# Set attention and a hard-swish layer on one core: the order and the issuers of the first loads, and half of a weight cast by a transfer

## The chip, the cores and the metric

The kernel runs on one core of one Trainium2 chip. The metric is the device time of one execution, in microseconds; lower is better. Time before: a median of 312.26 us over 6 runs (311.8 to 313.66).

## The reference

Two attention blocks with 32 inducing points, and then a feed-forward layer with a hard-swish, on x of 4 batches of 12480 tokens by 128 channels.

```
h   = mab(inducing, x)          # per batch: softmax over 12480 tokens, 32 x 128
y   = mab(x, h)                 # softmax over 32 points, 12480 x 128
mab(q, kv): a = softmax(q @ kv.T / sqrt(128));  return a @ kv
u   = y.reshape(49920, 128) @ w_in          # 128 x 2048
out = (u * clip(u + 3, 0, 6) / 6) @ w_out   # 2048 x 128
```

All inputs and the output are float32.

## The kernel before

The kernel does not run the layer over its 2048 hidden columns for each token. From each batch's 32 inducing outputs it makes small coefficient tables (a linear part BD and a quadratic part Cq), and per chunk of 512 tokens it multiplies features of the token by them. A path that computes everything directly stands at the end and is entered only where a test of the values fails.

A batch is cut into six groups of 2048 tokens (128 partitions by 16 tokens) and a small one of 192 tokens (48 partitions by 4, group NF = 6). For each batch there are two stages. The first reads the batch (casts x to bf16 as xb, transposes it on TensorE into pt, copies pt to xT, multiplies by the inducing points to s, takes the exponential a, and sums hnd += a x). The second makes the coefficients and then the output. For batches 1 to 3 the first stage is laid between the output steps of the batch before; for batch 0 it stands alone at the start, and this is where the change is made. The schedule is written out by hand: every engine runs its instructions in the order in which the program gives them.

The steps of the opening, in the order in which they appear, with their lines:

- L106: SyncE loads the table of inducing points into I_sb.
- L110 load_x: loads one group of x into a tile of type fp32r, by GpSimd's queue (L122), in one request or in two halves. L125 loads group 0 in halves. L164 builds the identity on GpSimd, and L165 then loads the small group and groups 1 to 5 in one go. Group 5 of batch 0 lies in an output buffer (tile x), the others in five buffers xr.
- L172 warm(n): n matmuls on zeros in TensorE. L181 transposes I_sb into I_T.
- L185 to L220: GpSimd writes constants (memsets, copies, an iota), and L229 load_weights loads w_in_r and w_out_r (1 MB each).
- L340 a_first: batch 0 goes through in pieces of half a group. The small group is the third of the 13 pieces. Per turn k, the loop does transpose(k + 1), weights(k) (s and its exponential, L378 and L385), cast(k + 3) and add(k - 1) (hnd, L392, and the running sums of a on VectorE, dacc, then dlast for the last four pieces). Five pieces before the end GpSimd folds dacc (L415). A group's buffer is given to a group of batch 1 once its last half has been added (load_next, L418); from group 2 on those loads are held back until load_held (L132), which waits with a small copy, seen, for one of the d transfers.
- L627 c_first: the coefficients of batch 0. ScalarE casts w_in to w_in_b in two halves and w_out to w_out_b in four quarters (cast_w, L637), between its squares sq (L579) of the products dpm (L568). TensorE accumulates cp (L588) from sq and w_out_b, block by block (16 blocks of 128 hidden columns); every fourth block's square is done by VectorE (L576, L577). SyncE spreads dk into the tiles d (L763).
- L905: the loop over the chunks, which writes out (L844).

Of the kernel before, what the change touches and what calls it, by code (L numbers as in the profile page):

```python
# [40 lines left out]
def kernel(  # L41
# [39 lines left out]
    with ExitStack() as es:  # L81
# [21 lines left out]


        I_sb = const.tile([M, C], FP32, name="I_sb")
        nc.sync.dma_start(I_sb[:, :], inducing[:, :])  # L106

        xs, xbs = {}, {}

        def load_x(b, g, cuts=(0, TG)):  # L110
            t0, p, n = groups[g]
            src = x[b, t0 : t0 + p * n, :].rearrange("(p i) c -> p i c", i=n)
            if n < TG:
                t = xlast.tile([P, n, C], FP32R, name="xl")
            elif b == 0 and g == XBUF:

                t = osp.tile([P, TG, C], FP32R, name="x5", tag="os")
            else:
                t = xin.tile([P, TG, C], FP32R, name="xr")
            for lo, hi in zip(cuts, cuts[1:]):  # L120
                lo, hi = min(lo, n), min(hi, n)
                nc.gpsimd.dma_start(t[:p, lo:hi, :], src[:, lo:hi, :])  # L122
            xs[(b, g)] = t

        load_x(0, 0, (0, 8, 16))  # L125

        held = []
        NF = NGR - 1 if rest else NGR
# [29 lines left out]
        def load_weights():  # L158
            w_out = moe_w_out.rearrange("(kb kp) c -> kp kb c", kp=P)
            nc.gpsimd.dma_start(w_in_r[:, :], moe_w_in[:, :])  # L160
            nc.gpsimd.dma_start(w_out_r[:, :, :], w_out)


        make_identity(nc, ident[:, :])  # L164
        for g in (NF, *range(1, XBUF + 1)):  # L165
            load_x(0, g, (0, 8, 16) if g in (1, XBUF - 1, XBUF) else (0, TG))
        wake = const.tile([P, 512], BF16, name="wake")
        nc.vector.memset(wake[:, :], 0.0)
        ident_b = const.tile([P, P], BF16, name="ident_b")
# [2 lines left out]
        def warm(n):  # L172

            wp = psF.tile([P, 512], FP32, name="wp", tag="fb")
            for _ in range(n):
                nc.tensor.matmul(wp[:, :], lhsT=wake[:, :P], rhs=wake[:, :])
# [3 lines left out]
        itp = psF.tile([P, 512], FP32, name="itp", tag="fb")  # L180
        nc.tensor.transpose(itp[:, :M], I_sb[:, :], ident[:M, :M])  # L181
        nc.vector.tensor_copy(I_T[:, :], itp[:, :M])
        warm(8)

        eng = nc.gpsimd  # L185
        ones = const.tile([P, P], FP32, name="ones")
# [5 lines left out]
        for q in range(4):  # L192
            eng.memset(blk_f[32 * q : 32 * q + 32, 32 * q : 32 * q + 32], 1.0)
            eng.memset(one4_f[32 * q : 32 * q + 32, q : q + 1], -1.0)
        blk = const.tile([P, P], FP32R, name="blk")
        eng.tensor_copy(blk[:, :], blk_f[:, :])
        one4 = const.tile([P, SL], FP32R, name="one4")
# [25 lines left out]
        def half_rows():  # L223
# [2 lines left out]
            nc.vector.tensor_scalar(half_of[:, :], half_of[:, :], 3.0, 1.0 / 12.0, op0=ALU.is_equal, op1=ALU.mult)  # L226
            nc.vector.tensor_scalar_add(half_of[:, :], half_of[:, :], -1.0 / 6.0)

        load_weights()  # L229


# [108 lines left out]
        def a_first():  # L340

            st = S[0]
            pieces = [(g, h, h + 8) for g in range(XBUF + 1) for h in (0, 8)]
            pieces.insert(2, (NF, 0, SL))
            last = len(pieces) - 1
            a1s = {}

            def cast(k):
                g, lo, hi = pieces[k]
                p = groups[g][1]  # L350
                if lo == 0:
                    xbs[(0, g)] = xbin.tile([P, TG, C], BF16, name="xb")
                xb, xf = xbs[(0, g)], xs[(0, g)]
                if hi - lo == 8 and (lo == 0 or k == last):
                    cuts = [(nc.scalar.copy, lo, lo + 4), (nc.vector.tensor_copy, lo + 4, hi)]
                else:
                    cuts = [(nc.scalar.copy, lo, hi)]
                for eng, i, j in cuts:
                    eng(xb[:p, i:j, :], xf[:p, i:j, :].bitcast(FP32))

            def transpose(k):
                g, lo, hi = pieces[k]
                t0, p, n = groups[g]
                step = 4 if k == last else 8
                for i in range(lo, hi, step):
                    j = min(i + step, hi)
                    pt = side_bank(0, [P, 1024], BF16, "pt")
                    for q in range(i, j):
                        nc.tensor.transpose(pt[:, (q - i) * p : (q - i + 1) * p], xbs[(0, g)][:p, q, :], ident_b[:p, :p])
                    eng = nc.scalar.copy if k == last and i > lo else nc.vector.tensor_copy  # L370
                    eng(st["xT"][:, t0 + i * p : t0 + j * p], pt[:, : (j - i) * p])

            def weights(k):
# [14 lines left out]
            def add(k):  # L388
                g, lo, hi = pieces[k]
                p, w, a1 = groups[g][1], (hi - lo) * M, a1s[k]  # L390
                for q in range(lo, hi):
                    nc.tensor.matmul(  # L392
                        st["hnd"][:M, :C],
                        lhsT=a1[:p, (q - lo) * M : (q - lo + 1) * M],
                        rhs=xs[(0, g)][:p, q, :],
                        start=(k == 0 and q == lo),
                        stop=(k == last and q == hi - 1),
                    )
                f = a1[:p, :w].bitcast(FP32)
                d = st["dacc"][:p, lo * M : hi * M]  # L400
                if g == 0:
                    nc.vector.tensor_copy(d, f)
                elif k == last - 3:
                    st["dlast"] = cst.tile([P, 8 * M], FP32, name="dlast")
                    nc.vector.tensor_copy(st["dlast"][:, :], f)
                elif k > last - 3:
                    nc.vector.tensor_add(st["dlast"][:, :], st["dlast"][:, :], f)
                    if k == last:
                        c_red(0, st["dlast"][:, :], P, 8)
                else:  # L410
                    nc.vector.tensor_add(d, d, f)
                if k == last - 4:
                    d = st["dacc"]
                    for h in (8, 4, 2, 1):
                        nc.gpsimd.tensor_add(d[:, : h * M], d[:, : h * M], d[:, h * M : 2 * h * M])  # L415
                    st.setdefault("dred", []).append(d[:, :M])
                if hi == groups[g][2]:
                    load_next(0, g)  # L418

# [16 lines left out]
        def c_red(b, src, p, n):  # L436
            st = S[b]
            st["reds"] = st.get("reds", -1) + 1
            dred = cst.tile([P, M], FP32, name=f"dred{st['reds']}")
            nc.vector.tensor_reduce(  # L440
                dred[:p, :], src.rearrange("p (s m) -> p m s", m=M), axis=AX.X, op=ALU.add
            )
            st.setdefault("dred", []).append(dred[:p, :])
# [183 lines left out]
        def c_first():  # L627
# [2 lines left out]
            nc.scalar.copy(w_in_b[:, : F // 2], w_in_r[:, : F // 2].bitcast(FP32))  # L630
            c_den(0)
            nc.scalar.copy(w_in_b[:, F // 2 :], w_in_r[:, F // 2 :].bitcast(FP32))
            c_HT(0)
            warm(2)

            def cast_w(i, j):
                nc.scalar.copy(w_out_b[:, i:j, :], w_out_r[:, i:j, :].bitcast(FP32))  # L637
# [16 lines left out]
            for jb in range(3, 7):  # L654
                sg(jb)
                cs(jb - 3)
            cast_w(8, 12)
            sg(7)
            b_f(0, 0)
            cs(4)  # L660
# [4 lines left out]
            c_hs(0)  # L665
            b_base(0, 0, 1)
            cs(6)
            cast_w(12, 16)
            sq(10)
            cs(7)  # L670
            sq(11)
# [445 lines left out]
```

## Time and profile before

| what | value |
|---|---|
| median of 6 runs | 312.26 us |
| the profiled execution | 313.36 us, its span 311.5 us |
| TensorE matmul busy | 299.0 us, 96% of the span |
| VectorE, ScalarE busy | 235.6 us, 231.8 us |
| GpSimd busy | 35.5 us |
| moved by transfers | 66.69 MB |
| granted TensorE clock, mean | 0.994 |

The span runs from the first to the last instruction; the execution's own time has a little around it. Times in the profile are those of one execution. A busy share is an average over the whole span, in which the opening of some 45 us is quite different from the rest. In the views of single instructions a row gives the start, the duration, the engine, the line, the operation and, in brackets, how long the engine had been idle and what it had waited for.

### The profile page before, as it was taken

To read this page: it belongs to the slowest core of one execution; us is meant where nothing else is said; L and a number is where in the kernel's file an instruction comes from. 1 tells how busy PE (TensorE), PEld (TensorE's weight loads), DVE (VectorE), ACT (ScalarE), POOL (GpSimd) and SP (SyncE) were. 2 spreads that over 40 slices of the span, in tenths; PEclk is the share of its full clock that TensorE was granted. 3 is DMA by queue.
4 is the path that set the end of the run, shared out by engine and by line. 5 is a ranking of instruction groups with operands and counts; after the bars stand their busy time and mean duration, and the time that the engine had idled before them with its cause. 6 is when DMAs were issued, how large, how long until landed. Compare 5 with 4: busy or idle time off the path is not lost.

```text
span 311.5 us, 9606 instructions
## 1 busy us (share of the span) xinstructions
PE 299.0 (96%) x3923; PEld 233.8 (75%) x3929; DVE 235.6 (76%) x543; ACT 231.8 (74%) x425; POOL 35.5 (11%) x82
## 2 busy tenths in 40 slices
PE   8899999999999999999999999999999999999991
PEld 3687678887676878888767877888867786777781
DVE  1797796977883868878796668787888487888882
ACT  3778999886589678886679849888658945777760
POOL 7611301021100010101100000100000001000000
PEclk9999999999999999999999999999999999999997
DMA  6999496998963452899965525555255335466672
GB/s 215 393 397 356 103 374 213 310 320 238 387 210 93 142 178 65 294 298 318 336 208 188 176 53 171 182 187 172 51 187 170 142 88 189 161 222 211 215 250 97
DMA packets 25089, 66.69 MB, mean 214 GB/s; under 512 B 3168, under 2 KB 17536, under 8 KB 19408
## 3 DMA queue, kind: packets, MB, share of 16 engines
q0 software_dynamic: 9232, 46.83, 43.6%
q1 hardware_dynamic: 15808, 19.19, 22.6%
q8 instruction: 32, 0.52, 0.7%
q14 instruction: 17, 0.14, 0.1%
HBM read 27.67 MB, written 25.56 MB: 171 GB/s over the span
## 4 chain that ended last, share of the span: by engine, by line
PE 74%; ACT 11%; DVE 5%; DMA 4%; issue 2%; POOL 1%; ACTq 0%; DVEq 0%; POOLq 0%
PE op L816 27%; PE bp L776 11%; PE op L800 7%; PE hnd L290 6%; ACT sq L579 6%; PE pt L268 5%; DMA xr<-in_x_dram 4%; PE cp L588 4%; PE s L276 2%; PE pp L747 2%; ACT TF L783 2%; PE ep L703 2%; PE sp L717 1%; PE dpm L568 1%; PE lp L540 1%
## 5 line engine op out<-in xcount | busy, mean ns | idle before, releaser
L783 ACT ACTIVATE TF<-bp 128x512 bf16<-128x512 f32 (+1 forms) x200 | 117.3, 599 | 38.7 <-PE rp L736 20.9
L816 PE MATMUL op<-Cq,TF 128*128 128x128 bf16 (+1 forms) x800 | 109.3, 223 | 0.0
L816 PE MATMUL op<-Cq,TD 128*128 128x128 bf16 (+1 forms) x800 | 105.9, 219 | 0.0
L832 DVE TENSOR_TENSOR os<-op,r_all 128x512 f32<-128x512 f32 (+1 forms) x100 | 68.4, 684 | 18.9 <-PE op L816 17.8
L816 PEld LDWEIGHTS <-TF 128*128 128x128 bf16 (+1 forms) x800 | 50.5, 98 | 33.5 <-issue 24.8
L776 PE MATMUL bp<-xT,W 128*128 128x512 bf16 (+1 forms) x197 | 74.0, 376 | 0.1
L792 DVE TENSOR_TENSOR TD<-TF,d 128x1024 bf16<-128x1024 bf16 (+1 forms) x100 | 66.8, 668 | 1.0 <-DMA d<-dk 0.6
L816 PEld LDWEIGHTS <-TD 128*128 128x128 bf16 (+1 forms) x800 | 61.4, 98 | 0.7
L800 PE MATMUL op<-BD,nf 128*128 128x512 f32 (+1 forms) x100 | 53.3, 533 | 0.5 <-DVE os L832 0.4
L579 ACT ACTIVATE sq<-dpm 128x512 bf16<-128x512 f32 x60 | 35.2, 641 | 4.3 <-PE dpm L568 2.0
L259 ACT CAST xb<-xr 128x1024 bf16<-128x1024 f32 x36 | 37.6, 1056 | 0.0
L737 DVE RECIPROCAL r_all<-rp 128x4 f32<-128x4 f32 (+1 forms) x100 | 17.7, 177 | 24.3 <-PE rp L736 23.9
L736 PE MATMUL rp<-one,nf 128*128 128x4 f32 (+1 forms) x100 | 34.5, 345 | 0.4
L269 DVE COPY xT<-pt 128x1024 bf16<-128x1024 bf16 (+1 forms) x42 | 25.8, 618 | 8.3 <-PE pt L268 7.8
L844 POOL DMA_DIRECT2D out_dram<-os x21 | 11.3, 537 | 142.7 <-DVE os L832 136.0
L290 PE MATMUL hnd<-xr,a 128*32 128x128 f32 x288 | 24.2, 226 | 0.0
L754 ACT ACTIVATE dk<-pp 128x512 bf16<-128x512 f32 (+1 forms) x28 | 15.7, 560 | 10.4 <-PE pp L747 10.4
L268 PE MATMUL pt<-ident_b,xb 128*128 128x128 bf16 x300 | 23.3, 218 | 0.0
L776 PEld LDWEIGHTS <-W 128*128 128x128 bf16 x200 | 19.5, 97 | 5.0 <-issue 3.4
L588 PE MATMUL cp<-w_out_b,sq 128*128 128x128 bf16 x256 | 22.7, 220 | 0.5 <-ACT sq L579 0.5
L568 PE MATMUL dpm<-dH,w_in_b 128*128 128x512 bf16 x62 | 22.7, 381 | 0.0
L510 PE MATMUL gp<-HTr,w_in_r 128*128 128x32 f32 x64 | 21.3, 358 | 0.3 <-ACT HTr L488 0.3
(127 smaller groups left out, 407.5 us busy)
## 6 DMA issues: line engine op xcount, KB each, us to landing
xr<-in_x_dram POOLq DMA_DIRECT2D x20, 1024.0 KB, 8.0
out_dram<-os POOLq DMA_DIRECT2D x18, 1024.0 KB, 4.4
d<-dk SPq DMA_DIRECT2D x96, 128.0 KB, 3.8
out_dram<-os SPq DMA_DIRECT2D x5, 1024.0 KB, 4.1
xr<-in_x_dram POOLq DMA_DIRECT2D x6, 512.0 KB, 5.6
x<-in_x_dram POOLq DMA_DIRECT2D x2, 512.0 KB, 13.5
w_in_r<-in_moe_w_in_dram POOLq DMA_DIRECT2D x1, 1024.0 KB, 13.5
w_out_r<-in_moe_w_out_dram POOLq DMA_DIRECT2D x1, 1024.0 KB, 16.3
```

What stands on the lines that cost most here:

```text
L259: eng(xb[:p, lo:hi, :], xs[(b, g)][:p, lo:hi, :].bitcast(FP32))
L268: nc.tensor.transpose(pt[:, (i - lo) * p : (i - lo + 1) * p], xb[:p, i, :], ident_b[:p, :p])
L290: nc.tensor.matmul(st["hnd"][:M, :C], lhsT=a1[:p, i * M : (i + 1) * M], rhs=xs[(b, g)][:p, i, :], start=(g == 0 and i == 0), stop=(g == NG ...
L579: nc.scalar.activation(sq[:, :], dpm[:, :], ACT.Square)
L588: nc.tensor.matmul(st["cp"][:, k * C : (k + 1) * C], lhsT=sq[:, k * P : (k + 1) * P], rhs=w_out_b[:, jc, :], start=(jc == 0 and k == 0), s ...
L736: nc.tensor.matmul(rp[:p, :SL], lhsT=nf[:, j * p : (j + 1) * p], rhs=one4[:, :])
L776: nc.tensor.matmul(bp[:, :w], lhsT=st["W"][:, k].rearrange("p m i -> p (m i)"), rhs=st["xT"][:, c0 : c0 + w],)
L783: nc.scalar.activation(st[("x", c)][:, k, :w], bp[:, :w], ACT.Exp, scale=scale)
L792: nc.vector.tensor_mul(u[:, :, :w], t[:, :, :w], d[:, :w].unsqueeze(1).to_broadcast([P, 2, w]))
L800: nc.tensor.matmul(op[:p, :], lhsT=st[("nf", g)][:, j * p : (j + 1) * p], rhs=st["BD"][:, :], start=True, stop=False, skip_group_check=True,)
L816: nc.tensor.matmul(op[:p, s * C : (s + 1) * C], lhsT=T[k][:, s * p : (s + 1) * p], rhs=st["Cq"][:, k, :], start=False, stop=(s == SL - 1 a ...
L832: nc.vector.tensor_mul(ot[:p, j * SL : (j + 1) * SL, :], op[:p, :].rearrange("p (s c) -> p s c", c=C), r_all[:p, b, c, :].unsqueeze(2).to_ ...
```

## The change

The opening gets another order of loads, and one half of a cast another place.

1. Group 0's first half is loaded by SyncE, as plain float32, into an output buffer x0. ScalarE and VectorE cast it from there to bf16, and VectorE copies it into the fp32r tile that TensorE reads for hnd. The table of inducing points is loaded by ScalarE's queue instead.
2. GpSimd loads the second half of group 0, builds the identity, loads the first half of group 1, writes half of its constants, loads the second half of group 1, writes the rest, and then loads groups 2 to 5 in halves, the small group, and the weights.
3. The small group becomes the last of the 13 pieces. The finer cuts that the last piece had stay with the last half of group 5. The folding of dacc on GpSimd now follows the first half of group 4 and not the second half of group 3.
4. The warming run behind the transpose of I_sb has 5 matmuls, not 8.
5. The second half of w_out_b (blocks 8 to 15) is made by a transfer from w_out_r to w_out_b on GpSimd's queue, which casts on the way; the two casts of ScalarE that did it go.

```diff
         I_sb = const.tile([M, C], FP32, name="I_sb")
-        nc.sync.dma_start(I_sb[:, :], inducing[:, :])
...
         def load_x(b, g, cuts=(0, TG)):
...
-            if n < TG:
+            if cuts[0]:
+                t = xs[(b, g)]
+            elif n < TG:
...
-                nc.gpsimd.dma_start(t[:p, lo:hi, :], src[:, lo:hi, :])
+                if (b, g, lo) == (0, 0, 0):
+                    x0 = osp.tile([P, TG, C], FP32, name="x0", tag="os")
+                    nc.sync.dma_start(x0[:, lo:hi, :], src[:, lo:hi, :])
+                    xs["x0"] = x0
+                else:
+                    nc.gpsimd.dma_start(t[:p, lo:hi, :], src[:, lo:hi, :])
             xs[(b, g)] = t
         load_x(0, 0, (0, 8, 16))
+        nc.scalar.dma_start(I_sb[:, :], inducing[:, :])
...
         make_identity(nc, ident[:, :])
-        for g in (NF, *range(1, XBUF + 1)):
-            load_x(0, g, (0, 8, 16) if g in (1, XBUF - 1, XBUF) else (0, TG))
+        load_x(0, 1, (0, 8))
...
-        warm(8)
+        warm(5)
...
             eng.memset(one4_f[32 * q : 32 * q + 32, q : q + 1], -1.0)
+        load_x(0, 1, (8, 16))
...
+        for g in range(2, XBUF + 1):
+            load_x(0, g, (0, 8, 16))
+        load_x(0, NF)
         load_weights()
...
-            pieces.insert(2, (NF, 0, SL))
+            pieces.append((NF, 0, SL))
...
-                if hi - lo == 8 and (lo == 0 or k == last):
+                if hi - lo == 8 and (lo == 0 or k == last - 1):
...
-                    eng(xb[:p, i:j, :], xf[:p, i:j, :].bitcast(FP32))
+                    eng(xb[:p, i:j, :], xs["x0"][:, i:j, :] if k == 0 else xf[:p, i:j, :].bitcast(FP32))
+                if k == 0:
+                    nc.vector.tensor_copy(xf[:, lo:hi, :], xs["x0"][:, lo:hi, :])
...
-                step = 4 if k == last else 8
+                step = 4 if k == last - 1 else 8
...
+                elif k < last - 3:
+                    nc.vector.tensor_add(d, d, f)
                 elif k == last - 3:
                     st["dlast"] = cst.tile([P, 8 * M], FP32, name="dlast")
                     nc.vector.tensor_copy(st["dlast"][:, :], f)
-                elif k > last - 3:
-                    nc.vector.tensor_add(st["dlast"][:, :], st["dlast"][:, :], f)
-                    if k == last:
-                        c_red(0, st["dlast"][:, :], P, 8)
                 else:
-                    nc.vector.tensor_add(d, d, f)
+                    nc.vector.tensor_add(st["dlast"][:p, :w], st["dlast"][:p, :w], f)
...
+                if k == last:
+                    c_red(0, st["dlast"][:, :], P, 8)
...
             nc.scalar.copy(w_in_b[:, F // 2 :], w_in_r[:, F // 2 :].bitcast(FP32))
+            nc.gpsimd.dma_start(w_out_b[:, FB // 2 :, :], w_out_r[:, FB // 2 :, :].bitcast(FP32))
             c_HT(0)
...
-            cast_w(8, 12)
             sg(7)
...
-            cast_w(12, 16)
             sq(10)
```

More of the change, by code (lines that the diff above doesn't have):

```diff
@@ L369, in transpose @@
                         nc.tensor.transpose(pt[:, (q - i) * p : (q - i + 1) * p], xbs[(0, g)][:p, q, :], ident_b[:p, :p])
-                    eng = nc.scalar.copy if k == last and i > lo else nc.vector.tensor_copy
+                    eng = nc.scalar.copy if k == last - 1 and i > lo else nc.vector.tensor_copy
                     eng(st["xT"][:, t0 + i * p : t0 + j * p], pt[:, : (j - i) * p])
```

## The prediction
> **What bounds the kernel now.** I read the page's slices first, then the chain that ended last for the first 60 us, then the order of time and the busy time by stretch over the same part.
>
> ```profile
> PE   8899999999999999999999999999999999999991
> ACT  3778999886589678886679849888658945777760
> DMA  6999496998963452899965525555255335466672
> ```
>
> TensorE is busy nearly everywhere, so the question is what stands ahead of its steady state. The busy time by stretch (sum, then PE, PEld, DVE, ACT, POOL, granted clock, DMA share, GB/s) splits the run:
>
> ```profile
> 3.00:21.70 18.70, 16.73 (x242) 12.85 (x242) 11.85 (x31) 12.12 (x22) 9.99 (x30) 1.00 1.09 385
> 27.88:38.98 11.10, 10.28 (x109) 7.52 (x111) 8.71 (x19) 10.61 (x22) 2.38 (x5) 1.00 0.61 179
> 45.00:290.00 245.00, 243.26 (x3213) 191.08 (x3213) 190.00 (x430) 187.59 (x345) 19.30 (x36) 1.00 0.62 200
> ```
>
> From 45 us on PE is busy 243.26 of 245.00 us. Whatever the opening of the kernel loses or wins arrives at the end one for one. The opening has two bounds: the transfers (share 1.09, 385 GB/s) while batch 0 comes in, and ScalarE (10.61 of 11.10 us) while the first coefficients are made. The chain (start, us, what) says the same:
>
> ```profile
> 3.57 2.64 POOL xr L122 x5
> 6.21 13.00 DMA xr<-in_x_dram
> 19.23 1.05 ACT xb L359
> ...
> 32.73 0.50 ACT w_out_b L637
> ...
> 35.20 0.50 ACT w_out_b L637
> ```
>
> Thirteen microseconds of the path are one wait for x. The last two casts of w_out are on the path as well, 0.50 us each.
>
> ```profile
> 0.76 0.40 SPq L106 DMA_DIRECT2D I_sb<-in_inducing_dram  x1
> 1.28 1.24 POOL L122 DMA_DIRECT2D xr<-in_x_dram  x2 [0.83 <-POOLq L1101]
> 12.71 0.62 ACT L359 CAST xb<-xr 128x512 bf16<-128x512 f32 x1 [1.17 <-DMA xr<-in_x_dram]
> 21.79 0.62 ACT L359 CAST xb<-x 128x512 bf16<-128x512 f32 x1
> 27.88 0.62 ACT L637 CAST w_out_b<-w_out_r 128x512 bf16<-128x512 f32 x1 [0.45 <-DMA w_out_r<-in_moe_w_out_dram]
> ```
>
> SP can issue at 0.76, GpSimd only at 1.28. The last half of group 5 was issued at 7.95 and took 13.8 us, so it landed near 21.7, and its cast follows at 21.79: it is still the transfers that decide when batch 0 ends. w_out lands at 27.88, just in time.
>
> **The change, part by part.** The sum is made against the profiled execution, 313.36 us (span 311.5 and 1.86 outside it), which is 1.1 above the median of 312.26.
>
> *Start of the stream.* By microseconds, the transfers moved 15 KB in 1 to 2, 46 in 2 to 3 and 229 in 3 to 4. The 15 KB are SP's inducing table (16 KB, landed 1.7 us after its issue), so a transfer issued by SP at 0.76 flows from about 1.9, one issued by GpSimd at 1.28 from about 2.9. The first half group gains 1.0 us at most, and nothing if its bytes only crowd out others. GpSimd then paces. Its work up to the first half of group 2 is one issue 0.62, the identity 0.54, one issue 0.53, the memsets 1.22 (8.44 to 9.66 in its row order), one issue 0.55 and the constants to the iota 1.32 (9.66 to 10.98): 1.28 + 4.78 = 6.06. Its bytes flow 1.6 after the issue, as the first load's did, at 7.7. Until 7.7 the stream of before had moved 1.63 MB; with the head start it would be at 2.0, and the four halves issued by then are 2.10 MB. So the stream just doesn't run dry; if each issue takes the slowest row's 0.70, it is dry for about 0.4. I take a head start of 0.9, nearer to the upper end because the 15 KB show SP's lead directly, and keep 0.2 and 1.0 as ends. The Trainium skill, "DMA: Bandwidth & Descriptors", section "Issuing engines are not separate DMA queues", speaks against the step: all issuers share the same 16 engines and a second one saves only issue time. By that rule alone the head start is SP's earlier issue, 0.52 us, and the sum 0.4 smaller.
>
> *The small group last.* Its 96 KB leave the way of group 5: at 385 GB/s that is 0.25. In return its work, hidden before in the waits for x, now stands at the end: PE's rows for it (transposes 0.27, s 0.27, hnd 0.42, pipelined) are about 0.65 from start to start. ScalarE's cast of 0.61 comes ahead of its half of the last evacuation and fits there because PE's transposes take that long. Batch 0 ended (last hnd) at 25.42, 3.63 after the cast at 21.79. Now: 21.7 - 0.9 - 0.25 = 20.55 for the landing, plus 0.09, 3.63 and 0.65, gives 24.9. Gain 0.5 to 0.6; I take 0.6, since VectorE's last add shrinks from 0.42 to 0.27. VectorE is the next bound: an evacuation 0.69, an add 0.42 and half of a 0.42 cast are 1.3 per half group, and nine halves from 10.4 (group 2 landing, 6.1 + the 4.3 that the first load took) end near 22, the same as the transfers within 0.5. GpSimd's folding of sums (four adds, 22.64 to 24.82) starts one half group later in the order and ends with the last hnd; it has 0.2 to spare.
>
> *What costs nothing.* The copy of x0 into its rounding tile is one VectorE copy of 1024 columns: 0.28 for 256 and 0.42 for 512 give 0.70, inside the wait for group 1. The evacuation of the first half now queues behind a cast that waits for group 1 (issue near 2.4, 4.3 to 5.3 to land: 6.7 to 7.7), so it runs at 7.1 to 8.1 against 7.78. Neither counts as long as group 2 ends the next wait; without that cover the copy costs 0.7. The I_sb issue on ScalarE (0.40) and its table load (1.28) end by 2.5, before any x. Three warming matmuls less free PE by 1.3 in a stretch where it waits for casts. On SP the d transfers stand 29 us later and see nothing.
>
> *w_out lands* at 27.88 - 0.9 = 27.0. Its first cast then ends at 27.6, before the first square needs ScalarE at 28.65 - 0.6 = 28.05. If the head start is lost but the rest is not, this wait takes 0.2 back.
>
> *Half of w_out by a transfer.* Two casts of 0.62 to 0.70 go, 0.50 each on the chain: 1.0. VectorE may take part of it. It ends nf at 33.61, waits 0.34 for PE, and then runs without a gap from 33.96 to 38.09; so its square for block 9 can move by 0.34 only, and the accumulation of block 9 with it. That one isn't the last wait, though: PE waited 0.22 for it and then 0.55 for ScalarE's square of block 10 (ended near 36.2), which moves by the whole 1.0. Bounds 0.4 and 1.0; I take 0.8, because ScalarE's idle time in that stretch (11.10 less 10.61) is small. The transfer must land before cp of block 8, at 34.92 before, 33.5 now. It is issued when w_out has landed and GpSimd's four adds are done, 27.0 to 27.6. Loads took from 2.4 (96 KB, empty queue) to 17.1 (full queue); two 1 MB loads of batch 1 are ahead of it, and the queue of before ran down to 57 GB/s by 31 to 32. I take 32, and 1.5 us of slack. Behind it on GpSimd waits only the seen copy, which waits for d until 36.56 anyway. The same page, section "Anatomy of one DMA", gives 2.0 us plus bytes at 436 GB/s; for 512 KB that is an estimate of 3.2 us, and by it the slack would be 2.7. No row of before shows such a transfer.
>
> Sum: 0.6 + 0.8 = 1.4. Profiled 311.96, median 312.26 - 1.4 = **310.9**.
>
> **Rivals.**
> *Late cast transfer (slower).* PE runs in order: if the transfer lands after 33.5, cp of block 8 stops it, and the dpm matmuls behind that feed ScalarE, one for one. The gain is gone at 34.9, and it is slower by 0.3% from 35.85. For it: w_out itself took 16.3 us from issue. Against: the queue is nearly empty by 31. Landing at 37 gives 312.26 + 2.1 = 314.4. Chance 0.13.
> *No head start.* The engines carry the same bytes at the same pace; only 0.25 is won and 0.65 lost at the end of batch 0. 0.8 - 0.4 = 0.4, or 0.8 where the small group hides: 311.5 to 311.9, say 311.6. For it: share 0.96 from 3 us on. Against: nothing moves before 2. Chance 0.2.
> *Pacing un-mixes the stream.* When group 5 landed at 21.7, 7.26 MB had moved, though x has 6.39: 0.87 MB of younger requests had passed. With halves one behind the other, half of that would be 0.43 MB or 1.1 us, of which VectorE lets 0.7 through, plus the other 0.2 of the casts: 2.3, 310.0. Chance 0.15.
>
> **How the numbers follow.** The forecast (310.3 to 311.5) has 0.5; 0.02 is for what I don't see, counted as slower. About 0.3%, 0.94 us, can be told from no change. Faster (below 311.3): 0.45 of the forecast, 0.15 of the third rival and 0.06 of the second, 0.66. Within it: 0.05 of the forecast, 0.13 of the second and 0.02 of a slightly late transfer, 0.2. Slower: 0.11 of the late transfer, 0.01 of the second and the 0.02, 0.14. The range runs from 309.3 (head start 1.0 and 0.25 with no cost at the end, 0.7 by un-mixing, 1.0 from the casts: 2.95) to 312.8, which takes in the late transfer up to a landing near 35.4.
>
> **What would show it.** In the changed profile: bytes near 200 GB/s before 2.9; the wait of the first cast of group 2 ending near 10.4 instead of 12.71; the last hnd ending near 24.9; w_out_b's first cast near 27.0; two w_out casts on ScalarE and no wait of cp for a transfer; TF of the first chunks 1.4 earlier than 38.98. I am wrong if the DMA share falls below 0.9 between 6 and 9, if the last landing of x doesn't move, or if cp waits for w_out_b.

## The result, and the profile after

The changed kernel is slower: a median of 315.14 us over 17 runs against 312.69 us over 38 runs of the kernel before beside them. The prediction had said 310.9, in a range from 309.3 to 312.8. The ratio, first measured, is 1.0066, 95% interval 1.005 to 1.0083; a second series gave 1.0059 (1.0036 to 1.0083). The profiled execution took 315.15 us (span 313.4); the one before took 313.36 (span 311.5).

The slices of the page hardly differ from those of before; 7.8 us in a slice is too coarse for an opening of 45 us:

```profile
PE   6879999999999999999999999999999999999992
ACT  3767999886579678887578949888658945777760
DMA  6999678988964443799985425654254345466672
```

The busy time by stretch of the changed kernel (columns as before: sum, PE, PEld, DVE, ACT, POOL, clock, DMA share, GB/s):

```profile
3.00:23.30 20.30, 15.69 (x231) 12.90 (x230) 12.34 (x30) 11.80 (x20) 11.08 (x31) 0.92 1.08 349
30.98:39.48 8.50, 8.19 (x89) 5.83 (x89) 6.72 (x14) 8.26 (x17) 0.19 (x2) 1.00 0.63 160
45.00:290.00 245.00, 243.26 (x3222) 191.57 (x3223) 190.06 (x431) 188.23 (x344) 19.35 (x36) 1.00 0.63 203
```

The first row, which ends where the last of x has come in, stood at 18.70 us before: x comes in 1.6 us later, at 349 GB/s against 385. The second runs from the first square to the product lp. Before, the same steps ran from 28.66 to 37.56, so 0.40 is won there:

```profile
28.66:37.56 8.90, 8.38 (x89) 5.84 (x89) 7.17 (x16) 8.90 (x19) 0.96 (x3) 1.00 0.53 161
```

The third is unchanged to the hundredth in PE. In the changed kernel the chain that ended last (start, us, what) still holds one wait of 13 us for x, now behind six issues of GpSimd:

```profile
6.49 3.30 POOL xr L128 x6
9.79 0.49 POOL x L128
10.28 13.01 DMA x<-in_x_dram
```

In the order of time, the changed kernel (start, us, engine, line, operation, idle before):

```profile
0.76 0.40 SPq L125 DMA_DIRECT2D x<-in_x_dram  x1
1.28 0.70 POOL L128 DMA_DIRECT2D xr<-in_x_dram  x1 [0.82 <-POOLq L1114]
4.74 0.62 ACT L370 CAST xb<-x 128x512 bf16<-128x512 f32 x1 [2.27 <-DMA x<-in_x_dram]
...
23.31 0.62 ACT L370 CAST xb<-x 128x512 bf16<-128x512 f32 x1 [0.18 <-DMA x<-in_x_dram]
...
29.88 0.62 ACT L652 CAST w_out_b<-w_out_r 128x512 bf16<-128x512 f32 x1
30.42 0.57 POOL L647 DMA_DIRECT2D w_out_b<-w_out_r  x1 [3.14 <-DMA w_out_r<-in_moe_w_out_dram]
...
45.90 0.68 DVE L845 TENSOR_TENSOR os<-op,r_all 128x512 f32<-128x512 f32 x1
```

The first cast and the first copy of an output in the kernel before:

```profile
5.61 0.62 ACT L359 CAST xb<-xr 128x512 bf16<-128x512 f32 x1 [3.58 <-DMA xr<-in_x_dram]
...
43.99 0.68 DVE L832 TENSOR_TENSOR os<-op,r_all 128x512 f32<-128x512 f32 x1
```

The first half group is cast at 4.74, where before it was 5.61: the start did come 0.87 earlier. The last half of group 5 is cast at 23.31, where before it was 21.79: by then 1.52 has been lost. The last row is the first copy of an output. It stood at 43.99 before; the shift of +1.91 stays between 1.85 and 1.94 over all 100 such copies. So three readings make up the whole loss in the opening: landing of x +1.52, from the last cast of group 5 to the last hnd +0.81 (4.44 against 3.63), casts of w_out -0.40. They sum to +1.93.

### The profile page after: what moved, and what is told of

It reads as the page before. It is cut to its first block, busy times and chain, and to the rows that moved or that the text cites. A ratio compares the mean times of both kernels' runs of the same rounds, so it can differ in the third digit from the quotient of the medians.

```text
span 313.4 us, 9606 instructions
## 1 busy us (share of the span) xinstructions
PE 298.5 (95%) x3921; PEld 234.1 (75%) x3926; DVE 237.2 (76%) x544; ACT 231.3 (74%) x423; POOL 37.1 (12%) x84
## 3 DMA queue, kind: packets, MB, share of 16 engines
q1 hardware_dynamic: 15904, 19.70, 23.2%
## 4 chain that ended last, share of the span: by engine, by line
PE 74%; ACT 9%; DVE 6%; DMA 4%; POOL 3%; issue 2%; ACTq 0%; DVEq 0%; POOLq 0%
PE op L829 27%; PE bp L789 12%; PE op L813 7%; PE hnd L301 6%; ACT sq L592 5%; PE cp L601 5%; PE pt L279 5%; DMA x<-in_x_dram 4%; PE s L287 2%; PE pp L760 2%; ACT TF L796 2%; PE dpm L581 2%; PE sp L730 2%; PE ep L716 2%; POOL xr L128 1%
## 5 line engine op out<-in xcount | busy, mean ns | idle before, releaser
L128 POOL DMA_DIRECT2D xr<-in_x_dram x27 | 14.8, 554 | 59.1 <-ACT TF L796 28.3
```

## The experiments

The changed kernel differs from the kernel before in five parts that could be set apart, and in the warming run, which e2 tries: kernels made from the changed one have 5 matmuls there, kernels made from the one before (and e12) 8. "SP": the first half group (and the copy, and the table on ScalarE's queue). "Halves": groups 2 and 3 in halves. "Paced": loads between GpSimd's constants. "Small": where the small group is requested and processed (third, fifth, or last of 13). "Cast": half of w_out_b by a transfer. The table gives, in us, the start of the last cast of group 5, the time from there to the end of the last hnd, that from the first square to lp, the shift of the first output copy against 43.99, and the ratio to the kernel before with its interval.

| run | SP | halves | paced | small | cast | last cast | tail | squares | shift | ratio |
|---|---|---|---|---|---|---|---|---|---|---|
| before | - | - | - | third | - | 21.79 | 3.63 | 8.90 | 0 | 1 |
| changed | x | x | x | last | x | 23.31 | 4.44 | 8.50 | +1.91 | 1.0066 (1.005 to 1.0083) |
| changed again | x | x | x | last | x | 23.30 | 4.44 | 8.50 | +1.90 | 1.0059 (1.0036 to 1.0083) |
| e2, warm 8 | x | x | x | last | x | 23.52 | 4.42 | 8.51 | +2.12 | 1.0036 (1.0015 to 1.0057) |
| e4 | x | x | x | last | - | 23.76 | 4.43 | 8.89 | +2.78 | 1.0081 (1.0052 to 1.011) |
| e3 | x | x | x | fifth | x | 22.85 | 3.64 | 8.50 | +0.66 | 1.0014 (0.9993 to 1.0034) |
| e1 | x | x | - | last | x | 22.38 | 4.43 | 8.50 | +0.98 | 1.0038 (1.0015 to 1.0061) |
| e10 | x | - | x | last | x | 22.03 | 4.56 | 9.35 | +1.83 | 1.0044 (1.0019 to 1.0069) |
| e18 | x | - | - | last | x | 22.31 | 4.42 | 8.50 | +0.92 | 1.005 (1.0028 to 1.0072) |
| e17 | x | x | - | fifth | x | 22.62 | 3.63 | 8.51 | +0.44 | 1.0027 (1.001 to 1.0045) |
| e8 | - | x | - | last | x | 22.75 | 4.57 | 8.51 | +1.49 | 1.0039 (1.0021 to 1.0058) |
| e11 | x | - | - | third | x | 20.64 | 3.80 | 8.50 | -1.41 | 1.001 (0.9982 to 1.0039) |
| e15 | x | - | - | third | x | 20.88 | 3.62 | 8.51 | -1.31 | 0.9973 (0.995 to 0.9996) |
| e5 | x | - | - | third | - | 21.69 | 3.62 | 8.89 | -0.12 | 1.0018 (0.9998 to 1.0037) |
| e6 | - | - | - | third | x | 21.74 | 3.63 | 8.50 | -0.47 | 0.9979 (0.9959 to 0.9999) |
| e16 | - | - | - | third | x | 21.48 | 3.63 | 8.51 | -0.70 | 0.9981 (0.9961 to 1.0) |
| e9 | - | x | - | third | - | 22.09 | 3.64 | 8.85 | +0.31 | 0.9984 (0.9966 to 1.0001) |
| e13 | - | - | x | third | - | 22.16 | 3.63 | 8.86 | +0.50 | 1.0011 (0.9991 to 1.0032) |
| e14 | - | x | x | third | - | 22.22 | 3.63 | 8.90 | +0.42 | 1.0012 (0.9993 to 1.0031) |
| e12 | - | - | - | last | - | 22.38 | 4.42 | 8.90 | +1.39 | 1.0027 (1.0004 to 1.005) |

The shift is a better measure of the opening than the time. From the start of the last output copy the same final instructions took 6.3 us in before and in the changed kernel, but 5.4 in e6, 5.2 in e9, 4.9 in e2 and 6.6 in e12, so the time differs by more than 1 us whatever the opening did. Each row has one profiled execution, and the landing varies among executions that request x in the same order: 21.48 to 21.79 (before, e6, e16), 23.30 to 23.76 (changed, changed again, e2, e4), but 20.64 to 21.69 (e5, e11, e15). A smaller difference than the spread of its kind is not read.

### First: four parts of the changed kernel

**e1_unpaced.** All requests for x stand directly behind the identity; nothing else changes.

```diff
-        load_x(0, 1, (0, 8))
+        for g in range(1, XBUF + 1):
+            load_x(0, g, (0, 8, 16))
+        load_x(0, NF)
...
-        load_x(0, 1, (8, 16))
...
-        for g in range(2, XBUF + 1):
-            load_x(0, g, (0, 8, 16))
-        load_x(0, NF)
         load_weights()
```

> The changed kernel, but GpSimd issues all halves of groups 1 to 5 and the small group straight after the identity, and the constants behind them. Theory (the stream ran dry because GpSimd issued late): from 4 to 12 us the stream moves about 400 GB/s as before and not 188 to 320, the last cast of group 5 starts near 21.3 instead of 23.31, and the time falls by 1.5 to 2 us against the changed kernel. Rival (SyncE's load crowds out GpSimd's bytes): the rate stays low between 5 and 8 us and the time falls by less than 0.5. Rival (the TensorE clock that sank to 0.5 in 10 to 12 us costs the time): the sinking goes only if the wait for x goes, the landing of group 5 stays.

Landing at 22.38, 0.93 sooner than in the changed kernel, but still 0.59 later than in the one before. So the pacing is a part of the loss and not the whole. Two stretches of 2 us by engine (the last column is GB/s, the one before it the DMA share); first before, then changed, then e1:

```profile
5.50:7.50 2.00, 2.00 (x11) 1.16 (x10) 0.43 (x1) 0.97 (x2) 1.38 (x4) 1.00 1.13 379
9.50:11.50 2.00, 1.85 (x35) 1.71 (x36) 1.29 (x5) 1.93 (x4) 1.94 (x8) 1.00 1.09 428
```

```profile
5.50:7.50 2.00, 0.85 (x9) 0.67 (x8) 0.39 (x1) 0.21 (x1) 2.00 (x5) 1.00 0.82 219
9.50:11.50 2.00, 1.71 (x28) 1.71 (x29) 1.26 (x3) 1.28 (x3) 1.35 (x3) 0.50 0.92 215
```

```profile
5.50:7.50 2.00, 1.55 (x10) 0.94 (x8) 0.54 (x1) 0.14 (x1) 1.19 (x2) 1.00 1.06 262
9.50:11.50 2.00, 1.69 (x32) 1.69 (x32) 1.54 (x3) 1.29 (x3) 0.54 (x2) 0.73 1.09 387
```

The changed kernel is slow in both, e1 in the first only. Nor is the first slow for want of requests: by 4.68 four halves (2.10 MB) had been requested, and at 8 us 1.63 MB had moved. In the second the DMA engines are 0.92 busy at 215 GB/s where they were 1.09 busy at 428: nearly the same busy time carries half the bytes. By the ratios the time fell by 0.7 to 0.9 us, and not by the 1.5 to 2 expected.

**e2_warm8.** The warming run is as long as before.

```diff
-        warm(5)
+        warm(8)
```

> The changed kernel with eight warming matmuls instead of five. Theory (late issue by GpSimd): the landings of x stay, the time is the same within 0.3 us. Rival (the granted clock of 0.5 to 0.7 between 9 and 13 us is the loss): the clock stays nearer to 1.0 and the time falls by 1 to 2 us.

TensorE's granted clock in 10 to 11 us, changed kernel and then e2:

```profile
10.00:11.00 1.00, 1.00 (x20) 1.00 (x17) 0.33 (x1) 0.78 (x2) 0.85 (x2) 0.50 0.87 188
```

```profile
10.00:11.00 1.00, 0.99 (x27) 0.99 (x28) 0.68 (x2) 0.59 (x2) 0.66 (x2) 1.00 0.87 217
```

The clock stays at 1.00 with the longer run, where TensorE waited 0.18 us for the second cast, and falls to 0.50 without it, where it had waited 2.04. But x comes in no sooner with it (a DMA share of 0.87 in both rows), the landing (23.52) and the shift (+2.12) are no better, so the clock cost nothing here. The time of e2 is nevertheless lower than that of the changed kernel, and not by its opening: its end was 4.9 us and not 6.3. Whether that is chance is open.

**e3_small_early.** The small group is requested behind group 1 and processed fifth.

```diff
+        load_x(0, NF)        # behind the second half of group 1
...
-        load_x(0, NF)        # behind group 5
...
-            pieces.append((NF, 0, SL))
+            pieces.insert(4, (NF, 0, SL))
```

> The changed kernel with the small group loaded behind group 1 and worked on as the fifth piece, not the last. Theory (its work at the end of batch 0 costs 0.65, its 96 KB ahead of group 5 cost 0.25 back): the tail from the last cast of group 5 to the last hnd shrinks from 4.4 to 3.6 us, the time falls by 0.4 to 0.8. Rival (it hides behind VectorE or GpSimd's folding of sums anyway): under 0.2.

The tail is 3.64 again, 0.80 less: the work of the small group is hidden as soon as it isn't last. The landing is 0.46 sooner, though 96 KB more stand ahead of it; that is as much as the spread. Together they bring the shift to +0.66 and the time to one that can't be told from before.

**e4_cast_back.** ScalarE casts all of w_out again.

```diff
-            nc.gpsimd.dma_start(w_out_b[:, FB // 2 :, :], w_out_r[:, FB // 2 :, :].bitcast(FP32))
...
+            cast_w(8, 12)
...
+            cast_w(12, 16)
```

> The changed kernel with ScalarE's two casts of the second half of w_out back in their places and no casting transfer. Theory (TensorE and VectorE take most of what ScalarE gives up): the time rises by 0.4, from the first square to the lp matmuls it takes 8.9 us as before instead of 8.5. Rival (the transfer disturbs the d transfers or the loads of batch 1): the time is the same or falls.

The squares take 8.89 and not 8.50: the transfer is worth 0.39. The rest of its shift is a landing 0.45 later, in a stretch that the edit doesn't touch; it is counted in the spread above.

### Second: one part alone on the kernel before

**a2_changed_again.** The changed kernel once more, for its spread.

> The changed kernel itself, beside the next three and the same runs of the kernel before. All theories: 1.5 to 2.5 us above the kernel before; its lp matmuls near 39.5 us.

The landing, the tail, the squares and the shift agree within 0.01. The way there doesn't agree so well: the first cast starts at 5.24 and not 4.74, and the two stretches of e1's rows run at 244 and 295 GB/s and not 219 and 215.

**e5_before_sp.** The kernel before, with the first half group by SP, the copy, and the table on ScalarE's queue.

```diff
-                nc.gpsimd.dma_start(t[:p, lo:hi, :], src[:, lo:hi, :])
+                if (b, g, lo) == (0, 0, 0):
+                    x0 = osp.tile([P, TG, C], FP32, name="x0", tag="os")
+                    nc.sync.dma_start(x0[:, lo:hi, :], src[:, lo:hi, :])
+                    xs["x0"] = x0
+                else:
+                    nc.gpsimd.dma_start(t[:p, lo:hi, :], src[:, lo:hi, :])
```

> The kernel before with one part alone: SyncE loads the first half of group 0 (with the copy by VectorE, the table of inducing points by ScalarE). Theory (the pacing starves the stream; SyncE's head start is worth its 0.25 MB): group 5 lands 0.6 us earlier than before and the time falls by 0.3 to 0.8. Rival (the SyncE transfer and what goes with it slows GpSimd's stream, which ran at 250 to 330 GB/s between 5.5 and 9 us even where nothing was paced): the stream has the same dip here, group 5 lands as late as before or up to 0.6 later, the time is the same or up to 0.6 longer.

The head start of the bytes holds here (3.74 MB moved at 12 us against 3.44, 6.84 against 6.52 at 20), but the last half of group 5 lands only 0.10 sooner.

**e6_before_cast.** The kernel before, with the casting transfer and without the two casts: e4's edit the other way round.

> The kernel before with the other part alone: the second half of w_out cast by a transfer, two casts fewer on ScalarE. Theory (TensorE is next behind ScalarE): from the first square to the lp matmuls 8.5 us instead of 8.9, the time falls by 0.4. Rival (nothing is gained because the transfer holds up the d transfers): no change, or the first TD product later than 38.95.

The squares fall by 0.40 and the time by 0.21% (0.01% to 0.41%). This part is a gain.

**e8_unpaced_nosp.** e1 with the first half group on GpSimd's queue again, and without the copy; the table of inducing points stays on ScalarE's queue.

```diff
-                if (b, g, lo) == (0, 0, 0):
+                if False:
```

> The unpaced kernel of the first study, with group 0 loaded by GpSimd alone (no x0, no copy). Theory (half requests are what slows the stream, not SyncE): rates of 250 to 330 between 5.5 and 9 us stay, the time is that of the unpaced kernel. Rival (SyncE's transfer slows it): rates of 370 and more from 5 us on as before, 12 us reached with 3.4 MB, and the time up to 0.6 shorter than the unpaced kernel's although the stream starts a microsecond later.

The first stretch is as fast as before (383 GB/s in 5.5 to 7.5 us), the landing is not (22.75). So SP's load, with its copy, is part of what makes e1's first stretch slow, and without it the order still loses: neither story, that SP alone or that pacing alone did it, stands.

### Third: pairs

**e9_before_halves.** On the kernel before, groups 2 and 3 in halves.

```diff
-            load_x(0, g, (0, 8, 16) if g in (1, XBUF - 1, XBUF) else (0, TG))
+            load_x(0, g, (0, 8, 16) if g < NF else (0, TG))
```

> The kernel before with groups 2 and 3 loaded in halves too, nothing else changed. Theory (two half requests move slower than one whole one early in the stream, as the 290 to 340 GB/s from 7 to 11 us of the unpaced kernel without SyncE's load suggest): the rate sinks to about 320 somewhere between 7 and 12 us, group 5 lands near 22.5 or later, the time rises by 0.7 to 1.5. Rival (the halves cost nothing; the slow stretch belongs to the order with the small group last): the time is the same within 0.3.

**e10_changed_whole.** The changed kernel with groups 2 and 3 in one request each.

```diff
-            load_x(0, g, (0, 8, 16))
+            load_x(0, g, (0, 8, 16) if g >= XBUF - 1 else (0, TG))
```

> The changed kernel with groups 2 and 3 loaded whole, as before; paced as in the changed one. Theory (pacing and halves both slow the stream): the time falls by about 1 against the changed kernel, group 5 lands near 22.4. Rival (pacing alone): no change, the stream stays near 2.8 MB at 12 us.

With halves alone the landing is 0.30 later, no more than the spread, and the time is not longer (0.9984): the 0.7 to 1.5 us that were expected aren't there. Taken out of the changed kernel they give 1.28 back, and both slow stretches are gone (404 and 397 GB/s). Only here does the stream run dry between the paced requests, the case that the prediction had priced at 0.4: by 8 us 269 GB/s had moved 2.15 MB, about all that had been requested before GpSimd's issues at 6.47. e10's stretch by engine:

```profile
8.00:9.00 1.00, 0.35 (x11) 0.36 (x12) 1.00 (x2) 0.18 (x1) 1.00 (x3) 0.99 0.74 197
```

e10's time gains little of this: its squares took 9.35 and not 8.50. TensorE's granted clock was low there, 0.85 over the stretch against 1.00 in the changed kernel, and a matmul of dpm took 0.61 us in place of 0.38 to 0.39:

```profile
30.00:32.00 2.00, 2.00 (x16) 0.76 (x13) 1.42 (x3) 1.60 (x3) 0.00 (x0) 0.50 1.08 316
```

**e11_sp_and_cast.** The kernel before with e5's and e6's edits.

> The kernel before with the two parts that cost nothing or gained: SyncE's first half group and the casting transfer. Theory (the parts add up): the casting transfer's 0.5 to 0.6 stay, SyncE's load adds nothing, 312.3. Rival (SyncE's load costs 0.7, as its mean against the kernel before said): 313.0.

**e12_before_small_last.** The kernel before, with the small group requested and processed last.

```diff
-        for g in (NF, *range(1, XBUF + 1)):
+        for g in range(1, XBUF + 1):
             load_x(0, g, (0, 8, 16) if g in (1, XBUF - 1, XBUF) else (0, TG))
+        load_x(0, NF)
...
-            pieces.insert(2, (NF, 0, SL))
+            pieces.append((NF, 0, SL))
...   # the finer cuts and the folding move as in the change
```

> The kernel before with the small group loaded and worked on last (and GpSimd's folding one half group later), nothing else changed; the constants behind the loads as before. Theory (its work at the end is on the path): from the last cast of group 5 to the last hnd 4.4 us instead of 3.6, group 5 lands up to 0.25 earlier, the time rises by 0.5 to 1.2. Rival (it costs only beside late loads): the same within 0.3.

In e11 the head start arrives: landing 1.15 sooner, shift -1.41; but its runs spread from 310.97 to 314.47, the profiled one (311.46) is the third fastest of the 12, and the ratio doesn't tell it from before. In e12 the small group last shifts the first output by what the sum of tail (0.79) and landing (0.59) says, +1.39: nothing is won by getting its 96 KB out of group 5's way.

### Fourth: pacing alone, and what is best

**e13_before_paced** and **e14_paced_halves.** The kernel before, paced as in the change, with groups 2 and 3 whole (e13) and in halves (e14).

```diff
-        for g in (NF, *range(1, XBUF + 1)):
-            load_x(0, g, (0, 8, 16) if g in (1, XBUF - 1, XBUF) else (0, TG))
+        load_x(0, NF)
+        load_x(0, 1, (0, 8))
...
+        load_x(0, 1, (8, 16))
         blk = const.tile
...
+        for g in range(2, XBUF + 1):
+            load_x(0, g, (0, 8, 16) if g >= XBUF - 1 else (0, TG))   # e14: (0, 8, 16)
         load_weights()
```

> The kernel before with GpSimd's requests paced between its constants as in the changed kernel, groups 2 and 3 whole, the small group and all else as before. Theory (the stream runs dry because requests come late, by itself): 12 us is reached with under 3.2 MB, group 5 lands 0.7 to 1.3 later than 21.75. Rival (late requests hurt only as halves): group 5 lands within 0.4 of before.

> The kernel before, paced and with groups 2 and 3 in halves. Theory (pacing decides; halves alone cost 0.3): group 5 lands 1.0 to 1.6 later than 21.75 and the first output is as much later. Rival (they need each other): 1.3 or more here, with under 0.4 for the pacing alone.

Without SP's load, the landing is 0.37 later with pacing and 0.43 with both, little more than the spread of 0.31, and neither time is told from before; e14 was expected to land 1.0 to 1.6 later. Only where SP's load is there too do the two go with the slow second stretch of the changed kernel (e14: 387 GB/s in 9.5 to 11.5).

**e15_sp_cast_again** and **e16_cast_again.** e11 and e6 once more.

> The kernel before with SyncE's first half group and the casting transfer, once more. Theory (the head start is real but its landing varies from execution to execution): group 5 lands anywhere from 20.6 to 21.7, the mean time lies near 313. Rival (the first profile was the rule): 20.6 again, and the time 1 us below the kernel before.

> The kernel before with the casting transfer alone, once more. Theory: 8.5 us from the first square to the lp matmuls, the time 0.4 to 0.6 below the kernel before. Rival (the first comparison was chance): no difference.

In the order of time and the stretches of e15, the fast counterpart of the rows above (its profiled run, 310.62, is the fastest of its 12, which reach 314.06):

```profile
20.88 0.62 ACT L363 CAST xb<-x 128x512 bf16<-128x512 f32 x1
...
42.68 0.68 DVE L837 TENSOR_TENSOR os<-op,r_all 128x512 f32<-128x512 f32 x1
```

```profile
5.50:7.50 2.00, 2.00 (x8) 0.82 (x7) 0.23 (x1) 1.26 (x2) 1.87 (x4) 1.00 1.15 359
9.50:11.50 2.00, 1.89 (x36) 1.64 (x37) 1.28 (x5) 1.97 (x4) 2.00 (x4) 1.00 1.07 422
```

The same SP load, and no slow stretch: the last cast 0.91 sooner than before, the first output 1.31 sooner. The casting transfer alone is faster than before in both series (0.9979 and 0.9981, the second with an interval that reaches 1); whether SP's load adds to it isn't settled by the two series of times (1.001 and 0.9973).

### Fifth: what is left between e15 and the changed kernel

**e17_changed_less_two.** e1 with the small group requested behind group 1 and processed fifth. **e18_small_last_left.** e1 with groups 2 and 3 whole.

```diff
# e17, against e1
         load_x(0, 1, (0, 8, 16))
+        load_x(0, NF)
...
-            pieces.append((NF, 0, SL))
+            pieces.insert(4, (NF, 0, SL))
# e18, against e1
-            load_x(0, g, (0, 8, 16))
+            load_x(0, g, (0, 8, 16) if g in (1, XBUF - 1, XBUF) else (0, TG))
```

> The changed kernel without the pacing and with the small group early (fifth piece, loaded behind group 1): SyncE's load, halves and the casting transfer are left. Theory (the parts cost mainly with one another): group 5 lands within 0.4 of the kernel with SyncE's load and the transfer alone (20.6 to 20.9), first output near 43. Rival (halves beside SyncE's load are what hurts, as the unpaced kernel's low rates from 5.5 to 9 us suggest): group 5 lands near 22 and the first output near 44.

> The changed kernel unpaced and with groups 2 and 3 whole: SyncE's load, the small group last and the casting transfer are left. Theory (the small group's tail of 0.8 is the only loss left, against a head start and 0.4 from the casts): tail 4.4 us, first output near 43.5 to 44. Rival (the order with the small group last also delays group 5 by 0.6, as it did alone): group 5 lands near 21.4 to 22, first output near 44.5.

e18 is e15 with the small group moved from third to last, and with 5 warming matmuls in place of 8. Its stretches:

```profile
5.50:7.50 2.00, 2.00 (x10) 1.02 (x9) 0.81 (x2) 0.58 (x2) 0.93 (x2) 1.00 0.85 238
9.50:11.50 2.00, 1.25 (x28) 1.25 (x29) 1.68 (x4) 1.13 (x3) 1.81 (x15) 0.88 1.06 420
```

The landing goes from 20.88 to 22.31, and the first stretch alone is slow; against e5, which requests x as e15 does and landed at 21.69, it is 0.62 later. e17 shows the same (262 GB/s, landing 22.62) with the request only two places further back, and with groups 2 and 3 in halves.

Over all twenty profiled executions, two conditions sort the slow stretches. In 5.5 to 7.5 us the rate is 207 to 262 GB/s in seven of the nine executions that have SP's load and no small-group request ahead of group 1 (the exceptions are e4 with 313 and e10 with 404); it is 346 to 359 in the three that have SP's load and that request, and 352 to 387 in the eight without SP's load. In 9.5 to 11.5 us it is 215 to 295 in all five executions with SP's load, halves and pacing together, and 311 or more in the other fifteen. So the loss needs combinations, and the parts don't add. Why a request of 96 KB ahead of group 1 goes with the faster stream is not settled: no run put another small request in its place.

These two windows are fixed, and a slow stretch elsewhere escapes them. The kernel before has one too, where the halves of group 4 follow the whole groups 2 and 3:

```profile
15.00:16.00 1.00, 1.00 (x23) 0.84 (x21) 1.00 (x4) 0.66 (x2) 0.00 (x0) 1.00 0.92 234
```

What the slow stretches share is the size of the packets, 4 KB for a half group and 8 KB for a whole one: in 9.5 to 11.5 us, 113 of 113 packets of the changed kernel are under 8 KB, and 4 of 108 before. In steps of 1 us from 5 to 20 over all twenty executions, 45 steps have at least 80% of their bytes in packets of 8 KB, and but for one step of e10, where its stream ran dry (197), none of them is below 360 GB/s. Of the 219 steps with at least 80% in packets of 4 KB, 35 are below 300, down to 188. So halves go with every slow stretch but that one; they don't make one by themselves, since the changed kernel's halves run at 410 GB/s in 12 to 14. x in whole groups throughout, behind SP's load or without it, was not tried.

The part "SP" holds two things that no run set apart: SP's load, and VectorE's copy of x0. In the seven executions that are slow in the first stretch the rate falls in 5.5 to 6.0, near that copy: in the changed kernel (copy from 5.21 to 5.89) 328 GB/s moved in 5.0 to 5.5 and 213 in 5.5 to 6.0. The Trainium skill, "SBUF — State Buffer", section "SBUF: two separate sides", has a rule that would explain it: while VectorE makes a float32 copy of this kind, GpSimd can't write the descriptors of the transfers that it issues, and they wait. What e18 lacks against e15 in the stretch, 121 GB/s for 2 us or 0.24 MB, is worth 0.67 us at e15's 359, about the copy's 0.70. Against it: the slow stretch outlasts the copy by some 1.5 us; the changed kernel run again had come down to 277 GB/s in 5.5 to 5.9 (393 in 5.0 to 5.5), before its copy began at 5.94; and e5, e11, e15 and e10 have the same copy at 4.85 to 5.92 without such a stretch. So the copy is a candidate and not shown; a first half group by SP without the copy was not tried.

## Why the prediction was wrong

*The failed step* is the landing of group 5: "So the stream just doesn't run dry", a head start of 0.9, and 0.25 for the small group's bytes gave 20.55 for the landing and 20.64 for the cast. It was 23.31. The arithmetic let the stream run at before's rate as long as anything was queued. Something always was, and the rate itself fell to 219 and 215 GB/s in two stretches. A head start of 0.27 MB at 5 us (0.85 against 0.58 moved) was a deficit of 0.63 MB at 12 (2.81 against 3.44). From 5 us to the landing the mean was 353 GB/s against 400; at 400 the 6.42 MB that moved in that time would have been through at 21.1 and not at 23.2. Why the rate falls stays open. The prediction had named the sign of this, a DMA share below 0.9 between 6 and 9 (it was 0.71 in 6 to 7 and 0.86 in 7 to 8), but priced pacing by the queue's content alone and gave splitting no cost. It also asked of the copy of x0 only whether VectorE had the time for it, and not what it might do to GpSimd's loads.

*The head start itself* was sized well. 229 GB/s moved in 2 to 3 us, where the prediction had awaited about 200 and before had 46; the first cast starts at 4.49 to 5.27 in the twelve executions with SP's load and at 5.55 to 5.88 in the eight without. With the order of requests of before it carried through to the cast of group 5 in two of three executions (e11 20.64, e15 20.88, against the 20.64 forecast; e5 21.69). Both of these were among the three fastest of their 12 runs, so how often it does is open. The rule of the Trainium skill, "DMA: Bandwidth & Descriptors", section "Issuing engines are not separate DMA queues", would have it at 0.52: those three gave 1.15, 0.91 and 0.10 and don't decide against it. The rule says nothing of what SP's load did in company, and that was the larger effect.

*The small group last* was forecast to gain 0.25 and lose 0.65. The tail lost 0.79 to 0.81 (e12, and e3 against the changed kernel), the right mechanism a little short. The gain has the wrong sign: with the request last, group 5 landed later, by 0.59 in e12, and in e18 by 0.62 to 1.67 against the three executions with SP's load and the order of before.

*The casts* gave 0.40 and not 0.8: e4, e6 and e16 agree. The bounds were 0.4 and 1.0, and the lower end was right. ScalarE lost its two casts, and TensorE became the bound, as the chain of the changed kernel shows in place of the casts:

```profile
34.75 0.32 PE sp L730
35.32 0.22 PE dpm L581
35.55 0.24 PE bp L789
35.79 0.22 PE cp L601 x4
```

The busy time by stretch says it as well: PE is busy 8.19 of the 8.50 us. I had argued from ScalarE's idle time alone and not asked how much TensorE had left: 0.52 of the 8.90 in the row of before. The waits of 0.22 and 0.55 that the prediction gave to PE were those of the weight loads (PEld); the matmuls themselves waited 0.22 there.

*The rivals.* The late transfer didn't happen. It was issued at 30.42 and took 5.5 us, to 35.9; the accumulation of block 8 started at 37.24 without a wait, 1.3 us later. The slack of 1.5 was right since both moved by the same. "No head start" was wrong about the cause and, at 311.5 to 311.9, about the sign. "Pacing un-mixes the stream" didn't happen: 7.3 MB had moved when the last of x landed, as before (314 GB/s to 23.2 us, 335 to 21.7). It named the right part and the wrong direction: pacing came with a landing 0.37 later on before and, out of the changed kernel, gave 0.93 back. No case priced a stream that is slowed by its own order of requests, and the slower side had one rival, at 0.13, and 0.02 for the unseen.

*What held:* the opening passes to the end one for one (+1.85 to +1.94 in the output copies, about +2.1 in the time by the ratio); w_out's landing moved with the stream (first cast at 29.88, 2.00 later); three warming matmuls fewer cost nothing that shows in the opening (e2); the copy of x0 took 0.68 of VectorE inside a wait.

## What to carry to other kernels

A stream of loads that is the bound has no fixed rate: read the GB/s of each short stretch and the size of its packets, and when requests are moved, split or given to another issuer, put a loss of rate in the range even if the queue never empties. Parts of a reordering that look independent (issuer, size, order, pacing) should be run apart; here the only part that could be shown to gain was the one that left the stream alone. When work is taken from a busy engine, the gain ends at the next engine's idle time in the same stretch: read that row before taking the middle of two bounds.

## What was not expected of the hardware

- The granted clock of TensorE fell to 0.50 in 9.5 to 11.5 us after an idle time of 2.04 us; with three more warming matmuls 5 us earlier it stayed at 1.00. No cost was seen, since the transfers were the bound. In e10 it fell to 0.50 in 30 to 32 us too, though no gap of TensorE between 22 and 29 us was longer than 0.32; there TensorE was the bound, and the squares took 0.85 longer.
- A copy of 32x128 on GpSimd took 0.75 us beside VectorE's copy of 1024 columns, and 0.28 in before, e1, e2 and e3. The Trainium skill, "SBUF — State Buffer", section "Who interferes with whom", tells of a port that VectorE shares with GpSimd and takes for itself in such copies; the two rows of the changed kernel agree with it:

```profile
5.21 0.68 DVE L372 CAST xr<-x 128x1024 fp32r<-128x1024 f32 x1
5.28 0.75 POOL L210 COPY sel<-ident 32x128 f32<-32x128 f32 x1
```

- A transfer from one tile to another in on-chip memory that casts 512 KB of float32 to bf16 took 0.57 us of GpSimd to issue and 5.5 us to land beside other traffic.
- The end of the kernel, with the same instructions, took from 4.9 us (e2) to 6.6 (e12); two executions of one kernel differed by up to 0.4 in it (e11 5.4, e15 5.0). No run shows why.
